# A linear-attention + feed-forward kernel: blocks of two batches, two tokens in each partition, and every engine's order from a list scheduler

## The chip, the cores and the metric

The kernel runs on one core of one Trainium2 chip. The metric is the time of one execution on the device in microseconds (us). A run is called slow when it is over 1.5% above the fastest of the same kernel, and fast runs are compared with fast runs. Each batch of experiments ran on one chip (by the record, chip 7, chip 14, and chip 4 for the last two), together with runs of the kernel before, whose median varied from 199.2 to 202.1 us between batches. So results of different batches are compared by their ratio to the kernel before of the same batch.

## The reference

A decayed linear attention ("RWKV-5"), whose output goes straight into a two-layer feed-forward part with a piecewise quadratic activation.

```python
# r, k, v: (4 batches, 8 heads, 768 tokens, 48); w, u: (8, 48)
for t in range(S):
    cur = einsum('bhd,bhe->bhde', u * k[t], v[t])
    y[t] = einsum('bhd,bhde->bhe', r[t], state + cur)
    state = w * state + einsum('bhd,bhe->bhde', k[t], v[t])
x = y.transpose(0, 2, 1, 3).reshape(3072, 384)
h = x @ w_in                                  # (384, 2048)
g = where(h >= 1, h, where(h <= -1, 0, (h + 1)**2 / 4))
return g @ w_out                              # (2048, 384)
```

The attention is computed in chunks of 128 tokens. Within a chunk, R is multiplied by powers of w and K by inverse powers, so that a plain product of R and K gives the decayed scores; a mask makes it causal; a state T carries what came before the chunk. For this data |h| stays under 1, so the activation is one squaring on ScalarE. A bound on norms is computed on the side, and a general path is run if it fails, which it never does here.

## The kernel before

The unit of attention is one batch and one chunk of 128 tokens, so a token is a partition. There are 24 units. Two of them make a block of 256 tokens for the feed-forward part, so there are 12 blocks.

```python
io = ctx.enter_context(tc.tile_pool(name="io", bufs=6))
...
man.enter_context(tc.block(schedule_with_timeline_sim=True))
units = [(b, c) for c in range(NCH) for b in range(B)]

def load():                       # one unit: 128 partitions, 8 runs of 192 bytes in each
    ...
    for name, src in (("K", k), ("R", r), ("V", v)):
        t = io.tile([128, H, D], F32, name=name, tag=name)
        nc.sync.dma_start(out=t, in_=src[b, :, t0 : t0 + C, :].rearrange("h s d -> s h d"))

def prep(i):
    nc.gpsimd.tensor_mul(Kw[:, :, 0:D], K, Winv)
    (nc.vector if i < 6 else nc.gpsimd).tensor_mul(Rw[:, :, 0:D], R, Wpow)
    nc.gpsimd.tensor_mul(KU, K, u3)
    nc.gpsimd.tensor_mul(KU, KU, R)
    ...                           # V to bf16
def s_tr(i):                      # R and K transposed: PE for the first 12 units, then by DMA
    if i >= TD:
        nc.sync.dma_start_transpose(RK, RKW[i % NR].rearrange("q h d -> q (h d)"))
        return
    ...
def s_y(i):                       # y = scores * V + R * state, then + V * diag, head by head
    ...
    for h in range(H):
        nc.vector.scalar_tensor_tensor(x[:, h*D:(h+1)*D], V[:, h, :], diag[:, h:h+1], y[:, h, :],
                                       op0=ALU.mult, op1=ALU.add)
    ...
def layer1(m, n):                 # 6 matmuls 128x256, then the squaring on ScalarE
def layer2(m, n):                 # 4 matmuls 128x384; at the end copy, and one 128-partition store
    ...
    nc.sync.dma_start(out=out[t0 : t0 + C, :], in_=o_sb)
# then a hand-written order: prep(0), prep(1), s_tr(0), s_at(0), ..., the steady state from a plan
```

Of the kernel before, what the change touches and what calls it, by code (L numbers as in the profile page):

```python
# [15 lines left out]
def kernel(  # L16
# [11 lines left out]
    nc = tc.nc  # L28
# [4 lines left out]
    NP = H // 2  # L33
    d_model = H * D
# [7 lines left out]
    NB = B * NCH // UB  # L42
    LIM = 0.95
    mm = nc.tensor.matmul

    const = ctx.enter_context(tc.tile_pool(name="const", bufs=1))
    stage = ctx.enter_context(tc.tile_pool(name="stage", bufs=4))
    io = ctx.enter_context(tc.tile_pool(name="io", bufs=6))
    work = ctx.enter_context(tc.tile_pool(name="work", bufs=3))
    gpool = ctx.enter_context(tc.tile_pool(name="gpool", bufs=3))  # L50
# [3 lines left out]
    ps_a = ctx.enter_context(tc.tile_pool(name="ps_a", bufs=4, space=bass.MemoryType.PSUM))  # L54

    man = ExitStack()
    man.enter_context(tc.block(schedule_with_timeline_sim=True))


    units = [(b, c) for c in range(NCH) for b in range(B)]  # L60
    loaded = {}
    next_load = [0]

    def load():
        i = next_load[0]
        if i == len(units):
            return
        next_load[0] += 1
        b, c = units[i]
        t0 = c * C  # L70
        tiles = []
        for name, src in (("K", k), ("R", r), ("V", v)):
            t = io.tile([128, H, D], F32, name=name, tag=name)
            nc.sync.dma_start(out=t, in_=src[b, :, t0 : t0 + C, :].rearrange("h s d -> s h d"))
            tiles.append(t)
        loaded[i] = tiles
# [4 lines left out]
    w_bc = const.tile([128, H * D], F32, name="w_bc")  # L81
    nc.sync.dma_start(out=w_bc, in_=row_bcast(w))

    wc = const.tile([128, NP], F32, name="wc")
    nc.vector.memset(wc, 1.0)
    with nc.allow_non_contiguous_dma(reason="384 words"):
        for s in range(2):
            nc.sync.dma_start(
                out=wc[s * DP : s * DP + D, :],
                in_=w.rearrange("(p s) d -> s d p", s=2)[s],  # L90
            )
    load()
    u_bc = const.tile([128, H * D], F32, name="u_bc")
    nc.sync.dma_start(out=u_bc, in_=row_bcast(u))
    load()

    w_in_sb = const.tile([128, nKb, d_ff], BF16, name="w_in_sb")
    w_out_sb = const.tile([128, nN, d_out], BF16, name="w_out_sb")
    NQ = 4
    FQ, TQ = d_ff // NQ, nN // NQ  # L100
    w_in_src = moe_w_in.rearrange("(ko ki) n -> ki ko n", ki=128)
    w_out_src = moe_w_out.rearrange("(no ni) d -> ni no d", ni=128)
    w_in_f, w_out_f = [], []
    for q in range(NQ):
        t = stage.tile([128, nKb, FQ], F32, name="w_in_f", tag="wf")
        nc.sync.dma_start(out=t, in_=w_in_src[:, :, q * FQ : (q + 1) * FQ])
        w_in_f.append(t)
        load()
    for q in range(NQ):
        t = stage.tile([128, TQ, d_out], F32, name="w_out_f", tag="wf")  # L110
        nc.sync.dma_start(out=t, in_=w_out_src[:, q * TQ : (q + 1) * TQ, :])
        w_out_f.append(t)


    ident = const.tile([128, 128], BF16, name="ident")
    make_identity(nc, ident)
    umask = const.tile([128, 128], F32, name="umask")
    nc.gpsimd.memset(umask, 0.0)
    nc.gpsimd.affine_select(
        out=umask, in_=umask, compare_op=ALU.is_ge, fill=1.0,  # L120
        base=0, pattern=[[-1, 128]], channel_multiplier=1,
    )
    ones = const.tile([128, 1], BF16, name="ones")
    nc.vector.memset(ones, 1.0)
    i_int = const.tile([128, 1], mybir.dt.int32, name="i_int")
    nc.gpsimd.iota(i_int, pattern=[[0, 1]], base=0, channel_multiplier=1)
    i_col = const.tile([128, 1], F32, name="i_col")
    nc.vector.tensor_copy(i_col, i_int)
    negj_col = const.tile([128, 1], F32, name="negj_col")
    nc.vector.tensor_scalar(negj_col, i_col, -1.0, -1.0, ALU.mult, ALU.add)  # L130
    lw = const.tile([128, H * D], F32, name="lw")
    nc.scalar.activation(lw, w_bc, AF.Ln)
    nc.scalar.activation(wc, wc, AF.Ln)
    Wpow = const.tile([128, H, D], F32, name="Wpow")
    nc.scalar.activation(Wpow.rearrange("p h d -> p (h d)"), lw, AF.Exp, scale=i_col)
    Winv = const.tile([128, H, D], F32, name="Winv")
    nc.scalar.activation(Winv.rearrange("p h d -> p (h d)"), lw, AF.Exp, scale=negj_col)  # L137
    nc.scalar.activation(wc, wc, AF.Exp, scale=float(C))
    u3 = u_bc.rearrange("p (h d) -> p h d", h=H)
    wc3 = wc[:, :, None].to_broadcast([128, NP, D])  # L140
    umask4 = umask[:, None, :].to_broadcast([128, NP, 128])



    NR = 4
    TD = 12
    RKW = []
    for i in range(NR):
        t = const.tile([128, 2 * H, DP], BF16, name=f"RKW{i}")
        nc.vector.memset(t, 0.0)  # L150
        RKW.append(t)

    T = [const.tile([128, NP, D], F32, name=f"T{b}") for b in range(B)]
    Tbd = []
    for b in range(B):
        nc.gpsimd.memset(T[b], 0.0)
        t = const.tile([128, NP, 2 * D], BF16, name=f"Tbd{b}")
        nc.gpsimd.memset(t, 0.0)
        Tbd.append(t)
    xT = [const.tile([128, UB, nKb, C], BF16, name=f"xT{m}") for m in range(NB)]  # L160
    xn = const.tile([128, len(units)], F32, name="xn")

    def pair(t, p):
        return t[:, 2 * p : 2 * p + 2, :].rearrange("q h d -> q (h d)")


    ut = {}

    def prep(i):
        K, R, Vf = loaded.pop(i)  # L170
        RK_w = RKW[i % NR]
        Rw, Kw = RK_w[:, 0:H, :], RK_w[:, H : 2 * H, :]
        nc.gpsimd.tensor_mul(Kw[:, :, 0:D], K, Winv)  # L173
        (nc.vector if i < 6 else nc.gpsimd).tensor_mul(Rw[:, :, 0:D], R, Wpow)
        KU = work.tile([128, H, D], F32, name="KU", tag="KU")
        nc.gpsimd.tensor_mul(KU, K, u3)  # L176
        nc.gpsimd.tensor_mul(KU, KU, R)  # L177
        V = work.tile([128, H, D], BF16, name="V", tag="V")
        if i < 8:
            nc.scalar.copy(V, Vf)  # L180
        else:
            nc.gpsimd.tensor_copy(V, Vf)  # L182
        ut[i] = [Rw, Kw, V, KU]

    def s_tr(i):
        Rw, Kw, V, KU = ut[i]
        RK = work.tile([128, 2 * NP, 128], BF16, name="RK", tag="RK")
        ut[i] = [Kw, V, RK, KU]
        if i >= TD:
            nc.sync.dma_start_transpose(RK, RKW[i % NR].rearrange("q h d -> q (h d)"))  # L190
            return
        tr = ps_a.tile([128, 2 * NP, 128], BF16, name="tr", tag="a")
        for p in range(NP):
            nc.tensor.transpose(tr[:, NP + p, :], pair(Kw, p), ident)  # L194
        for p in range(NP):
            nc.tensor.transpose(tr[:, p, :], pair(Rw, p), ident)  # L196
        nc.scalar.copy(RK, tr)  # L197

    def s_at(i):
        Kw, V, RK, KU = ut[i]  # L200
        RT, KT = RK[:, 0:NP, :], RK[:, NP : 2 * NP, :]
        AT_p = [ps_a.tile([128, NP, 128], F32, name=f"AT_p{s}", tag="a") for s in range(2)]
        for p in range(NP):
            for s in range(2):
                rows = slice(s * DP, s * DP + D)
                mm(AT_p[s][:, p, :], KT[rows, p, :], RT[rows, p, :], start=True, stop=True)  # L206
        AT = []
        for s in range(2):
            a = work.tile([128, NP, 128], BF16, name=f"AT{s}", tag=f"AT{s}")
            nc.vector.tensor_mul(a, AT_p[s], umask4)  # L210
            AT.append(a)
        diag = work.tile([128, H], F32, name="diag", tag="diag")
        nc.vector.reduce_sum(diag, KU, axis=mybir.AxisListType.X)  # L213
        load()
        ut[i] = [Kw, V, RT, AT, diag]

    def s_y(i):
        b, c = units[i]
        Kw, V, RT, AT, diag = ut[i]
        y = ps_a.tile([128, H, D], F32, name="y", tag="a")  # L220
        first = True
        if c > 0:
            for p in range(NP):
                mm(pair(y, p), RT[:, p, :], Tbd[b][:, p, :], start=first, stop=False, skip_group_check=True)  # L224
                first = False
        for h in range(H):
            mm(  # L227
                y[:, h, :], AT[h % 2][:, h // 2, :], V[:, h, :],
                start=first, stop=(h == H - 1), skip_group_check=True,
            )  # L230
            first = False
        if c < NCH - 1:
            st = ps_a.tile([128, NP, 2 * D], F32, name="st", tag="a")
            for p in range(NP):
                mm(st[:, p, :], pair(Kw, p), pair(V, p), start=True, stop=True)  # L235
# [5 lines left out]
        if c < NCH - 1:  # L241
            for s in range(2):
                rows = slice(s * DP, s * DP + D)
                part = st[rows, :, s * D : (s + 1) * D]
                if c > 0:
                    nc.vector.tensor_add(T[b][rows], T[b][rows], part)
                else:
                    nc.vector.tensor_copy(T[b][rows], part)
# [250 lines left out]
```

## Time and profile before

| | before |
|---|---|
| time, median of 3 runs | 200.65 us |
| span of the profiled run | 199.1 us |
| first layer-1 matmul | 25.03 us |
| first layer-2 matmul | 42.55 us |
| six layer-1 matmuls, four layer-2 matmuls, start to start | 0.655 us, 0.65 us |
| feed-forward work, 96 x 1.305 | 125.3 us |

Four lines of the page cut the span into 40 equal slices. A digit is the busy share of a slice in tenths (9 is 90% or more), and GB/s is what all 16 DMA engines of the core moved. From the page of the kernel before, with the count of packets, the queue of loads and stores, and the last column of the transfers, the us from issue to landing:

```profile
PE   0263598998989999999999959999999999999990
DMA  4999989999969999999999998334315022020202
GB/s 96 201 258 264 250 195 221 243 181 268 262 131 244 173 193 169 258 195 173 253 162 216 165 168 206 76 74 132 64 35 153 2 66 66 9 79 0 82 3 89
DMA packets 100444, 30.25 MB, mean 152 GB/s; under 512 B 93504, under 2 KB 98880, under 8 KB 100416
q1 hardware_dynamic: 100416, 29.90, 75.1%
K<-in_k_dram SPq DMA_DIRECT2D x24, 192.0 KB, 4.9
out_dram<-o_sb SPq DMA_DIRECT2D x24, 192.0 KB, 2.3
w_in_f<-in_moe_w_in_dram SPq DMA_DIRECT2D x4, 768.0 KB, 5.7
w_out_f<-in_moe_w_out_dram SPq DMA_DIRECT2D x4, 768.0 KB, 5.9
```

TensorE (PE) is full from about 60 us to the end, but for one slice. Next, the table of stretches of the kernel before (columns: window, its length, busy us with instruction counts of PE, weight loads, DVE, ACT and POOL, granted clock, mean DMA share, GB/s). A DMA share over 1 means that packets overlap on an engine.

```profile
20.00:40.00 20.00, 16.88 (x176) 12.87 (x178) 18.48 (x55) 16.74 (x36) 14.77 (x16) 1.00 1.01 228
60.00:80.00 20.00, 20.00 (x202) 14.67 (x202) 11.23 (x32) 12.31 (x25) 18.41 (x22) 1.00 1.17 194
100.00:120.00 20.00, 17.48 (x178) 12.29 (x177) 12.81 (x46) 10.52 (x25) 14.63 (x19) 0.92 1.17 177
120.00:140.00 20.00, 20.00 (x216) 14.62 (x214) 12.68 (x45) 12.65 (x28) 13.81 (x18) 1.00 0.52 119
```

And three rows of PE's timeline of the kernel before (start, us, engine, line, operation, out<-in, count, and in brackets the idle time just before it and what ended it):

```profile
25.03 2.77 PE L279 MATMUL h_p<-xT_195,w_in_sb 128*128 128x256 bf16 x12
42.55 1.58 PE L297 MATMUL o_p<-w_out_sb,gT 128*128 128x384 bf16 x8
116.52 2.52 PE L279 MATMUL h_p<-xT_201,w_in_sb 128*128 128x256 bf16 x12 [2.47 <-DMA xT_201<-x]
```

### The profile page before, as it was taken

The page shows a single profiled execution, that of the slowest core. Times are in us where ns is not written, and L with a number is a line of the kernel's source. Part 1 is how long each engine was busy: PE and PEld are TensorE (multiplying, and loading weights), DVE is VectorE, ACT ScalarE, POOL GpSimd, SP SyncE. Part 2 cuts the span into 40 slices and gives each one's busy share as a digit, 9 for nine tenths or more (in the row PEclk, how much of TensorE's full clock was granted, in tenths as well). Part 3 has the DMA queues.
Part 4 walks back from the last instruction along what each step waited for, and adds up shares of the span by engine and source line. Part 5 has one row for each costly group of instructions (what it writes and reads, how often), then busy time and mean ns, then how long its engine had stood idle before and what let it go on. Part 6 is the DMA issues. An engine that isn't in the chain of part 4 may idle for free.

```text
span 199.1 us, 4592 instructions
## 1 busy us (share of the span) xinstructions
PE 172.3 (87%) x1686; PEld 125.7 (63%) x1686; DVE 111.8 (56%) x354; ACT 122.0 (61%) x251; POOL 110.8 (56%) x144
## 2 busy tenths in 40 slices
PE   0263598998989999999999959999999999999990
PEld 0141476776867677866777547677667677777750
DVE  4179979994867608842867643776576464200110
ACT  3657769999887547936558326567555356454540
POOL 7496756989976999967679386857221000000000
PEclk9999999999999999999999979999999999999999
DMA  4999989999969999999999998334315022020202
GB/s 96 201 258 264 250 195 221 243 181 268 262 131 244 173 193 169 258 195 173 253 162 216 165 168 206 76 74 132 64 35 153 2 66 66 9 79 0 82 3 89
DMA packets 100444, 30.25 MB, mean 152 GB/s; under 512 B 93504, under 2 KB 98880, under 8 KB 100416
## 3 DMA queue, kind: packets, MB, share of 16 engines
q1 hardware_dynamic: 100416, 29.90, 75.1%
q8 instruction: 15, 0.25, 0.6%
q14 instruction: 13, 0.11, 0.2%
HBM read 20.84 MB, written 4.72 MB: 128 GB/s over the span
## 4 chain that ended last, share of the span: by engine, by line
PE 66%; DMA 5%; DVE 4%; ACT 2%; POOL 1%; issue 1%; ACTq 0%; DVEq 0%
PE o_p L297 28%; PE h_p L279 26%; DVE x L238 3%; DMA xT_201<-x 3%; DMA R<-in_r_dram 2%; PE y L227 2%; PE y L224 2%; PE st L235 1%; PE xp L265 1%; PE tr L194 1%; ACT gT L285 1%; ACT RK L197 1%; POOL RKW_173 L173 0%; POOL KU L177 0%; PE tr L196 0%
## 5 line engine op out<-in xcount | busy, mean ns | idle before, releaser
L285 ACT ACTIVATE gT<-h_p 128x512 bf16<-128x512 f32 x96 | 56.8, 598 | 44.9 <-PE h_p L279 42.6
L297 PE MATMUL o_p<-w_out_sb,gT 128*128 128x384 bf16 x384 | 73.5, 327 | 0.0
L279 PEld LDWEIGHTS <-w_in_sb 128*128 128x128 bf16 x576 | 54.5, 99 | 14.5 <-issue 3.4
L297 PEld LDWEIGHTS <-gT 128*128 128x128 bf16 x384 | 36.2, 98 | 19.3 <-issue 0.7
L238 DVE SCALAR_TENSOR_TENSOR x<-V,diag,y 128x48 bf16<-128x48 bf16 x192 | 35.8, 257 | 18.5 <-PE y L227 11.1
L176 POOL TENSOR_TENSOR KU<-K,u_bc 128x384 f32<-128x384 f32 x24 | 24.5, 1021 | 1.9 <-DVE diag L213 1.6
L177 POOL TENSOR_TENSOR KU<-KU,R 128x384 f32<-128x384 f32 x24 | 24.3, 1013 | 0.3
L301 DVE COPY o_sb<-o_p 128x384 f32<-128x384 f32 x12 | 6.7, 555 | 23.8 <-PE o_p L297 23.7
L197 ACT COPY RK<-tr 128x1024 bf16<-128x1024 bf16 x12 | 12.2, 1014 | 3.9 <-PE tr L196 3.8
L182 POOL CAST V<-V 128x384 bf16<-128x384 f32 x16 | 8.1, 503 | 11.3 <-DVE x L238 7.0
L206 PEld LDWEIGHTS <-RK 48*128 48x128 bf16 x192 | 8.3, 99 | 9.5 <-issue 4.2
L213 DVE TENSOR_REDUCE diag<-KU 128x8 f32<-128x384 f32 x24 | 13.1, 546 | 2.1 <-POOL KU L177 1.9
L265 PE MATMUL xp<-ident,x 128*128 128x128 bf16 x36 | 7.9, 236 | 5.6 <-DVE x L238 5.1
L301 ACT COPY o_sb<-o_p 128x384 f32<-128x384 f32 x12 | 5.7, 476 | 7.5 <-PE o_p L297 6.4
L173 POOL TENSOR_TENSOR RKW_171<-K,Winv 128x384 bf16<-128x384 f32 x6 | 6.0, 997 | 6.9 <-ACT Winv L137 3.5
L279 PE MATMUL h_p<-xT_201,w_in_sb 128*128 128x256 bf16 x48 | 7.4, 302 | 2.5 <-DMA xT_201<-x 2.5
L173 POOL TENSOR_TENSOR RKW_177<-K,Winv 128x384 bf16<-128x384 f32 x6 | 6.2, 1029 | 6.1 <-PE st L235 3.9
L265 PEld LDWEIGHTS <-x 128*128 128x128 bf16 x36 | 3.6, 101 | 8.9 <-DVE x L238 8.0
L194 PE MATMUL tr<-ident,RKW_171 128*128 128x128 bf16 x12 | 1.4, 249 | 8.8 <-POOL RKW_171 L173 8.8
L173 POOL TENSOR_TENSOR RKW_173<-K,Winv 128x384 bf16<-128x384 f32 x6 | 6.6, 1094 | 3.6 <-DMA K<-in_k_dram 1.8
L279 PE MATMUL h_p<-xT_195,w_in_sb 128*128 128x256 bf16 x48 | 7.7, 311 | 0.1
L173 POOL TENSOR_TENSOR RKW_175<-K,Winv 128x384 bf16<-128x384 f32 x6 | 6.4, 1072 | 2.1 <-DMA K<-in_k_dram 1.6
(356 smaller groups left out, 321.9 us busy)
## 6 DMA issues: line engine op xcount, KB each, us to landing
K<-in_k_dram SPq DMA_DIRECT2D x24, 192.0 KB, 4.9
R<-in_r_dram SPq DMA_DIRECT2D x24, 192.0 KB, 4.7
V<-in_v_dram SPq DMA_DIRECT2D x24, 192.0 KB, 4.9
out_dram<-o_sb SPq DMA_DIRECT2D x24, 192.0 KB, 2.3
w_in_f<-in_moe_w_in_dram SPq DMA_DIRECT2D x4, 768.0 KB, 5.7
w_out_f<-in_moe_w_out_dram SPq DMA_DIRECT2D x4, 768.0 KB, 5.9
w_bc<-in_w_dram SPq DMA_DIRECT2D x1, 192.0 KB, 3.5
u_bc<-in_u_dram SPq DMA_DIRECT2D x1, 192.0 KB, 4.3
```

Of the source, the lines that this page charges most:

```text
L173: nc.gpsimd.tensor_mul(Kw[:, :, 0:D], K, Winv)
L176: nc.gpsimd.tensor_mul(KU, K, u3)
L177: nc.gpsimd.tensor_mul(KU, KU, R)
L197: nc.scalar.copy(RK, tr)
L206: mm(AT_p[s][:, p, :], KT[rows, p, :], RT[rows, p, :], start=True, stop=True)
L213: nc.vector.reduce_sum(diag, KU, axis=mybir.AxisListType.X)
L238: nc.vector.scalar_tensor_tensor(x[:, h * D : (h + 1) * D], V[:, h, :], diag[:, h : h + 1], y[:, h, :], op0=ALU.mult, op1=ALU.add)
L265: nc.tensor.transpose(xp[:, kk, :], x[:, kk * 128 : (kk + 1) * 128], ident)
L279: mm(h_p[:, f, :], w_in_sb[:, kk, (2 * n + f) * 128 : (2 * n + f + 1) * 128], xT[m][:, :, kk, :], start=(kk == 0), stop=(kk == nKb - 1),)
L285: nc.scalar.activation(g, h_p, AF.Square, bias=0.5, scale=0.5)
L297: mm(o_ps[m][j], gT[m][:, f, j * C : (j + 1) * C], w_out_sb[:, f, :], start=(f == 0), stop=(f == nN - 1))
L301: (nc.scalar.copy if j else nc.vector.tensor_copy)(o_sb, o_ps[m][j])
```

## The change

The intent was threefold: fewer and longer DMA packets (384 bytes instead of 192), fewer and larger instructions on DVE and POOL (256 tokens in each), and an earlier, denser start, from an order that a list scheduler works out inside the kernel. A block is now two batches and one chunk. Batch b of the two lies on partitions 64b to 64b+63, with two neighbouring tokens in each partition, so each load and each store becomes two transfers of 64 partitions.

```diff
-    units = [(b, c) for c in range(NCH) for b in range(B)]
-    ...
-            t = io.tile([128, H, D], F32, name=name, tag=name)
-            nc.sync.dma_start(out=t, in_=src[b, :, t0 : t0 + C, :].rearrange("h s d -> s h d"))
+    blocks = [(c, b0) for c in range(NCH) for b0 in range(0, B, UB)]
+    half = [slice(b * HC, (b + 1) * HC) for b in range(UB)]          # HC = 64
+    def load(m, name):
+        c, b0 = blocks[m]
+        tl = io.tile([128, H, UB * D], F32, name=name, tag=name)
+        for b in range(UB):
+            nc.sync.dma_start(
+                out=tl[half[b]],
+                in_=src[b0 + b, :, c * C : (c + 1) * C, :].rearrange("h (p j) d -> p h (j d)", j=UB),
+            )
...
-        (nc.vector if i < 6 else nc.gpsimd).tensor_mul(Rw[:, :, 0:D], R, Wpow)
+        on_pool = name == "K" and m >= EARLY                           # EARLY = 3 blocks
+        (nc.gpsimd if on_pool else nc.vector).tensor_mul(to[:, js], src[:, js], tab[:, js])
...
-        for h in range(H):
-            nc.vector.scalar_tensor_tensor(x[...], V[:, h, :], diag[:, h : h + 1], y[:, h, :], ...)
+    # V*diag is a POOL product; PE adds it to y (3 early blocks), or DVE in four adds (the others)
...
-                nc.sync.dma_start(out=out[t0 : t0 + C, :], in_=o_sb)
+        for i in range(UB):
+            nc.sync.dma_start(out=out[t0 + i : t0 + C : UB, :], in_=t["o_sb", m, j][half[i]])
...
-    man.enter_context(tc.block(schedule_with_timeline_sim=True))
+    man.enter_context(tc.block())
+    man.enter_context(tc.manual_schedule())
+    P, L0 = 12.3, 16.0                              # us of a block; wished start of layer 1
+    for m in range(NB):                             # every operation: engine, us, needs, date, buffers
+        op(("ld", name, m), "SP", 1.55, (load, m, name), ...)
+        op(("tr", m), "SP", 3.1, (tr_dma, m), ...)
+        op(("xs", m), "ACT", 0.9, (xsq, m), [("x", m)], ..., start=27.0 if early else 0.0)
+        op(("L1", m, n), "PE", 0.66, (layer1, m, n), ...)
+        op(("L2", m, j, n), "PE", 0.33, ..., [...("xT", EARLY - 1)...])   # not before block 2's x
+    ...
+    while left:                                     # take the most urgent of what can start next
+        ...
+    # and dummy matmuls into unused PSUM in PE's idle time of the first 40 us, to keep its clock up
```

Scores, y and state are twice as many half-array matmuls, since the two halves of the partitions are different batches. Only 3 of 12 blocks are transposed on PE, instead of 12 of 24 units. The feed-forward matmuls stay as they were.

## The prediction

> **What bounds the kernel now.** TensorE, but not all the time. In the timeline six layer-1 matmuls (128x256) take 0.655 us start to start and four layer-2 matmuls (128x384) 0.65, so the feed-forward part needs 96 x 1.305 = 125.5 us. By the same view one attention unit costs PE about 1.0 us for scores, y and state, and 0.6 more where PE transposes (12 of 24 units). With the weight norms I estimate 158 us of PE work in a span of 199. By the table of stages PE is full from 60 us on, but for 2.5 us at 111 us, where layer 1 waits for the transposing DMA into xT_201 (chain of waits). The other ~38 us: the first layer-1 matmul starts at 25 us; 25 to 60 us has short gaps while ACT is 90% and DVE 80% busy and 192-byte loads saturate the DMAs; the last matmul (193.7) is followed by 5.4 us of copy, store and end. The first twelve layer-1 matmuls take 2.6 us, twice their later time, though the granted clock reads 1.00. The Trainium skill ("TensorE: Matmul & The Clock Gate", part 1) says an idle PE runs at half clock until some 3.4 us of activity; the trace agrees.
>
> **What changes.** Feed-forward matmuls stay.
> - Loads have 384-byte runs: 36,864 packets, not 73,728, same bytes. "DMA: Bandwidth & Descriptors" (why small descriptors are slow) names a fixed cost per packet; I expect the loads to land sooner while DMA is saturated.
> - V*diag+y, eight DVE instructions per unit (0.19 us start to start), becomes PE adds or four DVE adds per block plus a POOL product. Masks halve in number, not in elements. POOL stays near 10 us per block; ACT is near full from 10 to 40 us.
> - PE transposes remain for 3 of 12 blocks, not 6: 3 to 4 us of PE saved, more DMA transposes.
> - Scores, y and state become twice as many half-array matmuls; if two overlap, as the score pairs do now (starts 0.01 us apart), about 2.2 us per block against 2.0: +2 us.
> - Dummy matmuls keep the clock up: 1.5 us gained.
> - The order: layer 1 is to start near 16 us.
>
> **On the critical path.** First layer 1 near 17 us, not 25. Layer 2 cannot start before block 2's transpose, about 32 us, with some 8 us of layer 1 done. Left then: 117.5 feed-forward + 9 blocks x 2.2 - 0.8 (no last states) + 1.6 norms = 138 us; 32 + 138 = 170, + 3 of waits, + 5.4 end = 178.5 span, + 1.5 (time minus span, before) = 180.
>
> **Prediction:** 180 us, range 174 to 189. Faster by over 2%: 0.93; within 2%: 0.04; slower: 0.03.
>
> **Seen in the profile if right:** first layer-1 matmul at 15 to 19 us, at full rate; first layer-2 matmul at 30 to 36; layer groups still 0.65; no PE hole over 2 us after 45 us; attention 2.0 to 2.5 us of PE per block; 66 PE transposes of data, not 132; load packets halved; end still about 5 us.
>
> **What would make it wrong.** Half-array matmuls that don't overlap, or drain PE at each switch: up to +20. DVE and POOL slowing each other (DVE's R product took 0.56 to 1.35 us), so that the fixed order stalls; POOL over 12.5 us per block would be the limit. ACT late with block 2: each us there is one at the end. Loads that don't speed up: +4. A denser start and 2.0 us per block: 174.

## More of the kernel before

Loads are issued from one queue, the SP engine's, and so are the transposing transfers and the stores.

The twelve matmuls at 25 us take 2.77 us, nearly twice what twelve take later (1.49 us at 28.6 us). The twelve after the one hole, from 114.05 to 116.52 us, where PE waited 2.47 us for a transposing transfer (the prediction puts this hole at 111 us), take 2.52 us. The trace has the granted clock at 0.50 there, from 116.8 to 120.1 us.

## The result

The changed kernel is slower: 213.22 us median (211.97, 212.94 and 213.50 fast, 216.08 slow) against 200.63 (199.09 to 200.88) in the same rounds. The ratio of the fast runs is 1.0751, 95% interval 1.0643 to 1.0859. A ratio in this document is the record's: the mean time of one kernel's fast runs over that of the other's fast runs of the same rounds, so it is not quite the ratio of the medians quoted. For this pair the runs listed don't give it: their fast means are 212.80 and 200.31 us, a ratio of 1.062, just under the recorded interval. A size that rests on 1.0751 is uncertain by 1%, and is given below as a range.

The page of the changed kernel (span 210.1 us), the same lines as above:

```profile
PE   7769949999899859994979894979999999999980
DMA  5999999999999998999999998992570220503042
GB/s 118 202 204 332 221 241 268 242 211 213 249 181 187 161 184 186 198 195 163 207 199 172 205 180 182 155 180 60 51 164 3 52 65 0 115 0 75 3 100 64
DMA packets 72224, 32.49 MB, mean 155 GB/s; under 512 B 65280, under 2 KB 70656, under 8 KB 72192
q1 hardware_dynamic: 72192, 32.06, 83.7%
K<-in_k_dram SPq DMA_DIRECT2D x24, 192.0 KB, 5.3
out_dram<-o_sb SPq DMA_DIRECT2D x48, 96.0 KB, 2.2
w_in_f<-in_moe_w_in_dram SPq DMA_DIRECT2D x4, 768.0 KB, 10.3
w_out_f<-in_moe_w_out_dram SPq DMA_DIRECT2D x4, 768.0 KB, 8.2
```

There are 28,000 packets fewer, and yet the queue's packets now fill 83.7% of a longer span instead of 75.1%. DMA is full to about 142 us instead of 120. No load lands sooner (medians of K, R and V: 5.3 to 5.6 us, and 4.7 to 4.9 before), and the quarters of w_in take 10.3 us instead of 5.7. The 7s at the start of PE's row are mostly dummy matmuls. The table of stretches of the changed kernel:

```profile
20.00:40.00 20.00, 16.46 (x285) 13.80 (x282) 15.20 (x17) 15.19 (x29) 7.20 (x5) 0.91 1.17 240
60.00:80.00 20.00, 16.72 (x281) 11.52 (x280) 14.57 (x20) 9.53 (x21) 11.69 (x9) 1.00 1.21 186
100.00:120.00 20.00, 18.61 (x268) 13.30 (x262) 14.55 (x19) 11.27 (x23) 12.10 (x10) 1.00 1.14 195
120.00:140.00 20.00, 15.49 (x201) 10.74 (x200) 11.72 (x18) 10.52 (x23) 13.95 (x9) 0.91 0.99 179
```

Between 60 and 80 us PE was full before (20.00) and is now 16.72, while DVE, ACT and POOL are all less busy than 15 of 20 us. No compute engine is full there, but the DMA share is 1.21. PE's timeline of the changed kernel shows the start and three of the holes:

```profile
23.87 1.47 PE L370 MATMUL h_p<-xT,w_in_sb 128*128 128x256 bf16 x12
47.95 0.81 PE L390 MATMUL o_p<-w_out_sb,gT 128*128 128x384 bf16 x4
76.01 1.16 PE L370 MATMUL h_p<-xT,w_in_sb 128*128 128x256 bf16 x9 [3.11 <-DMA xT<-x]
99.73 0.52 PE L338 MATMUL st<-Vb,RKW 64*128 64x96 bf16 x16 [2.95 <-DVE AT L259]
129.36 0.64 PE L254 MATMUL A<-RK 48*64 48x128 bf16 x16 [2.89 <-DVE wsq L441]
129.94 1.46 PE L390 MATMUL o_p<-w_out_sb,gT 128*128 128x384 bf16 x4
```

The dummies did their part: the first twelve layer-1 matmuls take 1.47 us, not 2.77, although the granted clock fell to 0.50 once more later (30.1 to 33.4 us). But they start at 23.87 us, not near 17, and layer 2 starts at 47.95, not near 32.

The hole before 76.01 shows how a full DMA queue gets to PE. The two views below are the timeline of the SP queue (the time that issuing took, waiting for room or for data included) and that of POOL, both of the changed kernel:

```profile
50.00 9.66 SPq L244 DMA_TRANSPOSE RK<-RKW  x2
62.27 1.35 SPq L187 DMA_DIRECT2D K<-in_k_dram  x2
69.19 2.34 SPq L323 DMA_TRANSPOSE xT<-x  x1
```
```profile
67.26 1.82 POOL L199 TENSOR_TENSOR RKW<-K,Winv 128x768 bf16<-128x768 f32 x1 [7.05 <-DMA K<-in_k_dram]
```

Two transposing transfers hold the queue for 9.66 us, so the next K is issued at 62.27, and POOL sits idle for 7.05 us until it has landed. The transposing transfer of x sits in the same queue behind four stores and eight loads; x is ready at 67.2, its transfer is issued at 69.19, and PE gets its input at 76.01. Over the whole span, the waits of the changed kernel hold two lines for loads (columns: us in total, times, longest). Before, the same waits add up to 8.4 us for K, in four lines because the tiles were numbered there, and 3.1 us for R:

```profile
POOL RKW L199 <- DMA K<-in_k_dram: 11.8, 3, 7.0
DVE RKW L199 <- DMA R<-in_r_dram: 9.7, 5, 3.2
```

The trace also has a record of every DMA packet. I grouped those of the queue of loads, stores and transposes by size (mean ns that a packet took, and their sum per engine of 16):

```
                 192/384-byte loads   256-byte transposes   1536-byte stores,    2048-byte      sum,
                 ns    us/engine      ns    us/engine       w_out: ns  us/eng    w_in: ns       us/engine
before          18.9    87.3         24.4   25.8            74.9   25.2          101.2          149.6
after           37.1    85.6         28.2   44.7            97.0   32.6          111.3          175.8
```

Here a packet of twice the bytes takes twice as long (37.1 against 18.9 ns), so the loads cost the queue what they cost before, 86 us per engine. The stores cost more, although their bytes are the same, and the transposes cost 19 us more, most of it because there are more of them. That is the reading that the experiments had to explain.

### The profile page after: what moved, and what is told of

It is laid out like the page before. It is cut to its first block, busy times and chain, and to the rows that moved or that the text cites. A ratio compares the mean times of both kernels' runs of the same rounds, so it can differ in the third digit from the quotient of the medians.

```text
span 210.1 us, 5752 instructions
## 1 busy us (share of the span) xinstructions
PE 182.0 (87%) x2427; PEld 135.8 (65%) x2427; DVE 111.5 (53%) x148; ACT 112.7 (54%) x221; POOL 102.7 (49%) x80
## 3 DMA queue, kind: packets, MB, share of 16 engines
q1 hardware_dynamic: 72192, 32.06, 83.7%
HBM read 20.84 MB, written 4.72 MB: 122 GB/s over the span
## 4 chain that ended last, share of the span: by engine, by line
PE 47%; DMA 16%; DVE 11%; SPq 9%; ACT 6%; issue 4%; POOL 4%; DVEq 0%; POOLq 0%; ACTq 0%
PE o_p L390 19%; PE h_p L370 16%; SPq L187 6%; DMA K<-in_k_dram 5%; DVE RKW L199 4%; PE w_p L149 4%; DMA xT<-x 3%; DMA w_out_f<-in_moe_w_out_dram 3%; DVE x L305 3%; DMA R<-in_r_dram 3%; PE A L254 2%; ACT gT L379 2%; DVE AT L259 2%; DMA V<-in_v_dram 2%; SPq L244 2%
## 5 line engine op out<-in xcount | busy, mean ns | idle before, releaser
L370 PE MATMUL h_p<-xT,w_in_sb 128*128 128x256 bf16 x576 | 78.2, 276 | 3.8 <-DMA xT<-x 3.1
L259 DVE TENSOR_TENSOR AT<-A,umask 128x1024 bf16<-128x1024 f32 x24 | 28.2, 1218 | 18.0 <-PE A L254 18.0
L207 POOL TENSOR_TENSOR KU<-K,u_bc 128x768 f32<-128x768 f32 x12 | 23.2, 1936 | 9.7 <-DVE x L305 4.6
L199 DVE TENSOR_TENSOR RKW<-R,Wpow 128x768 bf16<-128x768 f32 (+1 forms) x13 | 22.0, 1700 | 10.0 <-DMA R<-in_r_dram 9.7
L210 POOL TENSOR_TENSOR KU<-KU,R 128x768 f32<-128x768 f32 x12 | 25.6, 2134 | 1.3 <-DMA R<-in_r_dram 0.5
L199 POOL TENSOR_TENSOR RKW<-K,Winv 128x768 bf16<-128x768 f32 x9 | 16.3, 1808 | 19.6 <-DMA K<-in_k_dram 11.8
L305 DVE TENSOR_TENSOR x<-y,KU 64x384 bf16<-64x384 f32 x36 | 20.0, 555 | 9.0 <-PE y L282 4.6
L149 PE MATMUL w_p<-ident 128*128 128x128 bf16 x251 | 20.2, 244 | 1.9 <-POOL ident masks.py:199 1.4
L149 PEld LDWEIGHTS <-ident 128*128 128x128 bf16 x251 | 17.9, 112 | 2.8 <-POOL ident masks.py:199 1.4
L223 POOL TENSOR_TENSOR KU<-V,dg 128x768 f32<-128x768 f32 x9 | 13.5, 1500 | 4.0 <-DVE dg L214 3.0
## 6 DMA issues: line engine op xcount, KB each, us to landing
w_in_f<-in_moe_w_in_dram SPq DMA_DIRECT2D x4, 768.0 KB, 10.3
```

Source lines behind the costliest of these rows:

```text
L149: mm(w_p[:, 0:128], ident, ident, start=True, stop=True)
L199: (nc.gpsimd if on_pool else nc.vector).tensor_mul(to[:, js], src[:, js], tab[:, js])
L207: nc.gpsimd.tensor_mul(t["KU", m], t["K", m], ub4)
L210: nc.gpsimd.tensor_mul(t["KU", m], t["KU", m], t["R", m])
L223: nc.gpsimd.tensor_mul(t["VD", m], t["V", m], dg)
L259: nc.vector.tensor_mul(a.rearrange("q s p t -> q (s p) t"), t["A", m, j].rearrange("q s p i t -> q (s p) (i t)"), umask4[j])
```

## The experiments

Theory 1: a transfer that covers only 64 partitions runs at a part of the rate of one that covers 128, and this takes back all that the longer runs gained. The Trainium skill states the first half of it on the page "SBUF — State Buffer", section "Door 1: The DMA port swizzle": partitions 0 to 63 reach 8 of the 16 ports, and the page measured 196 against 328 GB/s at 1 MiB. A later section ("Can I just issue two DMAs to hit both halves?") answers no, since two such transfers serialize. I had not looked there before predicting.

Rival 2: the order is wrong for the chip, because the list reckons with too short transfers. Rival 3: the start is bound by the compute engines (ScalarE's queue, DVE and POOL slowing each other, the dummies), and the late start costs its length. Fifteen kernels were run.

### 1. The transfers by themselves (m1_dma)

A kernel with no computation moves the same 4.72 MB six times, in transfers of six shapes, one after the other, and then stores. Its output is wrong, which doesn't matter for the time.

```python
# A: 128 partitions, 192-byte runs          B: two halves of 64 partitions, 384-byte runs
# C: 128 partitions, 384-byte runs          D: two halves, 192-byte runs
# E: 128 partitions, one 3072-byte run each F: two halves, one 3072-byte run each
for i, (x, b, c) in enumerate(jobs):        # C, for example
    nc.sync.dma_start(out=big[i], in_=x[b, :, c*128 : c*128+256, :].rearrange("h (p j) d -> p h (j d)", j=2))
```

> Six ways to move the same 4.7 MB of K, R and V, one after the other, nothing else running (output zero, wrong on purpose): A 128 partitions with 192-byte runs, B two halves of 64 partitions with 384-byte runs, C 128 partitions with 384-byte runs, D halves with 192-byte runs, E 128 partitions with 3072-byte runs, F halves with 3072-byte runs; then stores of 1536-byte rows, whole and in two interleaved halves. Theory 1[...]: C moves at 1.5 to 2 times the rate of B, B about as fast as A, D at half of A, F at half of E, half stores slower than whole ones. Rival 2 (under 512 bytes a packet costs in proportion to its bytes, whatever the partitions): B and C alike, A and D alike. Rival 3 (a packet has a fixed cost, and 384-byte packets were slow in the kernel only because of transposes and weights beside them): B twice as fast as A.

The rows of DMA and GB/s of this run's page have 40 slices of 4.2 us:

```profile
DMA  5999995999949995778877775994999966916664
GB/s 107 218 213 206 205 187 126 242 233 232 233 84 321 325 323 159 132 141 140 150 143 144 146 135 199 364 412 160 242 246 247 246 154 243 324 53 158 148 159 97
```

The plateaus are, in order, A, B, C, D, E, F and the stores. From the first issue of one phase to that of the next:

| shape | 192-byte runs | 384-byte runs | 3072-byte runs |
|---|---|---|---|
| 128 partitions | A 24.3 us, 194 GB/s | C 16.7 us, 282 GB/s | E 14.9 us, 317 GB/s |
| two halves of 64 | D 35.5 us, 133 GB/s | B 23.1 us, 204 GB/s | F 22.5 us, 210 GB/s |

The longer run is worth a factor of 1.45 (A to C), and the half width costs a factor of 1.4 (C to B) to 1.5 (E to F). The change went from A to B, across the diagonal, and the two nearly cancel: 194 to 204 GB/s. Stores of half width took 17 us where whole ones took 8, for the same 2.36 MB.

Two cautions. A shape in halves also has twice as many transfers here (B 24, C 12), and this run doesn't separate the two; A and B have 24 each. And D and the half stores are no clean measure of width: their DMA tenths are 7 to 8 and 6, not 9, so the DMA engines were not full (D's 48 transfers were issued 0.67 us apart). The packets themselves took 15.6 ns (A), 31.9 (B), 22.2 (C), 16.7 (D), 129 (E) and 201 (F), and those of the stores 68.2 whole and 100.5 in halves. So the direction of theory 1 holds for transfers alone, but the factor of 1.5 to 2 that I expected for B and C came out at 1.4. What it is worth in the kernel is another question.

### 2. Loads over all partitions, data wrong (e1_heads)

The changed kernel with each load's pair of transfers cut by heads, not by partitions. It has the same number of transfers, the same bytes and the same runs, but the tile then holds other data, so the output is wrong. Half-width stores remain.

```diff
-                out=tl[half[b]],
-                in_=src[b0 + b, :, c * C : (c + 1) * C, :].rearrange("h (p j) d -> p h (j d)", j=UB),
+                out=tl[:, hs],                               # hs: 4 of 8 heads
+                in_=src[b0, hs, c2 * C : (c2 + 2) * C, :].rearrange("h (p j) d -> p h (j d)", j=UB),
```

> The changed kernel, but each pair of load DMAs splits the tile by heads and not by partitions: both fill all 128 partitions, with 256 tokens of one batch (wrong data on purpose). Same number of DMAs, same 192 KB each, same 384-byte packets, same order on every engine. Theory 1[...]: the 384-byte packets fall from 37 ns to 20 to 25, loads land in 3 to 4 us and not 5.6, PE holes after 58 us shrink, the time falls from 213 to about 190 (180 to 198). Rivals 2 and 3 (bytes, or the order): packets stay at 35 to 37 ns, time 208 to 215.

It took 200.79 us (ratio 0.9984, 0.9877 to 1.0091, against 1.0751). The load packets took 26.0 ns instead of 37.1 (expected: 20 to 25), K landed in 4.8 us (expected: 3 to 4), and the queue's sum fell from 175.8 to 146.2 us per engine. The time fell by less than I expected of theory 1: it missed 190 by about 10 us and lies outside the 180 to 198 stated. The first layer 2 was still at 43.5 us. So the width is a large part of the loss, and not all of it.

### 3. No loads after the third block (e3_noload)

The later blocks reuse the tiles of the first three (output wrong). This takes 54 of 72 load transfers away.

```diff
+        if m >= 3:
+            t[name, m] = t[name, m - 3]
+            return
```

> The changed kernel without the K, R, V loads of blocks 3 to 11 (they use the tiles of blocks 0 to 2 again; wrong on purpose), transposes and stores kept. If DMA capacity is what gates blocks 3 to 11, PE has no hole over 2 us after 60 us and the time is 180 to 190. If the fixed order or the transposes alone gate them, it stays above 200.

It took 197.65 us (0.9861, 0.9765 to 0.9957), again short of the expected 180 to 190. From 60 us on PE has no hole over 1.1 us, and from the first layer 2 (45.9 us) to the end of the span it takes 148.5 us, where the prediction's sum has 138 + 3 + 5.4 = 146.4. So with the DMA freed the second part runs nearly as predicted, and what is missing lies before 50 us. That splits the error into two parts: the steady part, which DMA limits, and the start.

### 4. The list told what transfers really take (e4_est)

```diff
-            op(("ld", name, m), "SP", 1.55, ...        -            op(("tr", m), "SP", 3.1, ...
+            op(("ld", name, m), "SP", 2.1, ...         +            op(("tr", m), "SP", 4.0, ...
-        op(("li", q), "SP", 2.4, ... (and "lo")        -    LAND = 1.1
+        op(("li", q), "SP", 4.1, ... (and "lo")        +    LAND = 3.5
```

> The changed kernel with the scheduler told what the trace shows of DMA: a 384 KB load 2.1 us instead of 1.55, landing 3.5 us later instead of 1.1, weights 4.1 instead of 2.4, transposes 4.0 instead of 3.1. Same work, other order, result right. If a wrong order costs the time (rival), it comes down by 10 us or more, to 195 to 203. If DMA capacity costs it, it stays within 4 us of 213.

It took 215.87 us, ratio 1.0733 (1.0643 to 1.0822), the same as the changed kernel. Better estimates make another order, and it gains nothing. Rival 2 falls in this form.

### 5. DVE without POOL beside it (e5_pool)

The R*Wpow products on DVE took 0.95 us alone and up to 2.57 us beside POOL products, 1.70 in the mean. The Trainium skill ("SBUF — State Buffer", section "Who interferes with whom") says that a DVE instruction with two SBUF inputs contends with a GpSimd instruction that reads SBUF, and not with one that only writes it. So in the three early blocks I put two write-only fills in place of each of the three POOL products. The output passes the comparison, because that term is small.

```diff
     def ku1(m):
         t["KU", m] = work.tile([128, H, UB, D], F32, name="KU", tag="KU")
+        if m < EARLY:
+            nc.gpsimd.memset(t["KU", m], 0.01)
+            nc.gpsimd.memset(t["KU", m], 0.01)
+            return
         nc.gpsimd.tensor_mul(t["KU", m], t["K", m], ub4)       # ku2 and vdiag likewise
```

> The changed kernel, but the GpSimd products of the first three blocks (K*u, *R, V*diag) are memsets of the same tiles, which read no SBUF (wrong on purpose). Theory S1 (VectorE's products of two SBUF operands wait for GpSimd's, which doubles them on the way to the first layer 2): the DVE weighting products of blocks 0 to 2 fall from 2.6 us to 0.95, the first layer-2 matmul comes at 40 to 42 us instead of 46, the time falls by 3 to 6 us. Rival (the start is set by ScalarE, the dummies or the loads): the products shorten, but first layer 2 and time move by under 2 us.

The DVE products of the early blocks fell to 0.95 us, which agrees with the page, and the first layer 1 came at 20.61 us, 3.3 us earlier. The first layer 2 moved by 1.5 us only (46.47 us; the profile is of a slow run), and the time did not follow: 211.62 us in the one fast run, 215.19 to 216.12 in the three slow ones (so no ratio is given). PE then waited for quarters of w_out until 60 us. The contention is real: the products at 9.3, 14.2 and 16.0 us ran beside fills. But a fill takes 0.74 us where a product takes 1.5 to 2.6, and it waits for no load, so this run doesn't separate the contention from the shorter POOL work; together they cost 3 us of the first layer-1 date, and nothing of the total that shows.

### 6. No dummy matmuls (e6_nodummy)

```diff
-    WARM_END = 40.0
+    WARM_END = 0.0
```

> The changed kernel without the dummy matmuls. Theory S2 (the 41 dummies between scores and y of block 0 take 3.4 us where the scheduler reckons 2.3, so they hold up the real work): y of block 0 starts at about 16.5 us instead of 17.7, but the first layer-1 matmuls run at half speed; net -2 to +2 us. If the dummies are what keeps the clock up, the first layer-1 groups take 1.3 us instead of 0.66 and the time grows by 2 to 4 us.

It took 212.93 us (ratio 1.0684, 1.0561 to 1.0808; two of its four runs are slow). The first twelve layer-1 matmuls took 3.08 us instead of 1.47, so the dummies do keep the clock up. In the total they neither help nor hurt by more than the spread of the runs.

### 7. and 8. Full width with right data (v1, v1s)

To have full-width loads with right data, the block becomes one batch and two consecutive chunks (256 tokens). Two neighbouring tokens stay in a partition, partitions 0 to 63 hold the first chunk and 64 to 127 the second, and one transfer of 384 KB brings all of it. The state of the first chunk is handed to the second within the block. Version v1s also writes the activation's output in token order, so that a store is one transfer of 128 partitions.

```diff
-    blocks = [(c, b0) for c in range(NCH) for b0 in range(0, B, UB)]
+    blocks = [(c, b) for c in range(0, NCH, UB) for b in range(B)]       # first of two chunks, batch
-        for b in range(UB):
-            nc.sync.dma_start(out=tl[half[b]], in_=src[b0 + b, ...])
+        nc.sync.dma_start(
+            out=tl, in_=src[b0, :, c * C : (c + UB) * C, :].rearrange("h (p j) d -> p h (j d)", j=UB))
...                                                  # state added, decayed and cast once per chunk
# v1s:
-        for i in range(UB):
-            nc.sync.dma_start(out=out[t0 + i : t0 + C : UB, :], in_=t["o_sb", m, j][half[i]])
+        nc.sync.dma_start(out=out[t0 : t0 + C, :], in_=t["o_sb", m, j])
```

> A right version with full-width loads: a block is one batch and two chunks of 128 tokens that follow each other, so 256 tokens lie two to a partition over all 128 partitions and one DMA of 384 KB loads them; the second chunk's state comes from the same block. The rest as in the changed kernel. If the half-width loads cost what the run with loads split by heads says, it is near 200 (195 to 206), right, with 384-byte packets of 26 ns.

> The same, and ScalarE writes the hidden layer in token order, so that each output tile is stored by one DMA from 128 partitions instead of two from 64. Store packets (1536 bytes) fall from 97 to about 75 ns, some 7 us of every DMA engine's time; the last store ends 0.5 us sooner. Time 0 to 4 us below v1, unless ScalarE's strided writes are slower (hidden-layer activation over 0.65 us).

Both outputs are right. v1 took 203.09 us (1.0228, 1.0137 to 1.0318) and v1s 199.32 (1.0001, 0.9915 to 1.0086), on the same chip. The whole stores are worth 3.8 us (their packets went from 98.0 to 75.2 ns), net of what they cost: written in token order, the activation on ScalarE takes 746 ns instead of 594, over the 0.65 us that the expectation had named as the danger. In the same step the feed-forward work done by 49 us fell from 11.1 to 9.7 us; no run shows whether the activation did that. The later versions all keep this write. After 56 us v1s has no PE hole over 0.6 us. Its start is still slow: first layer 1 at 26.7 us, first layer 2 at 50.4.

### 9. to 12. The start (e7_xs, e8_early2, v2, v3)

Two things hold layer 2 back. One is the written rule that it may not start before the x of the last early block is transposed (they share PSUM buffers). The other is ScalarE's queue in front of that. e7_xs takes the squares of x of the early blocks (3 us of ScalarE work, needed only for the norm bound) out of the start. e8_early2 transposes only two blocks on PE, so that the rule refers to block 1. v2 and v3 apply both, or the first alone, to v1s.

```diff
# e7_xs (and v3, with 4 buffers of x):
-    RING = dict(..., x=2, ...)
+    RING = dict(..., x=5, ...)
-        op(("xs", m), "ACT", 0.9, (xsq, m), [("x", m)], d + 12 if early else d + 9, start=27.0 if early else 0.0)
+        op(("xs", m), "ACT", 0.9, (xsq, m), [("x", m)], d + 40 if early else d + 9, start=60.0 if early else 0.0)
# e8_early2 (and v2, beside the squares):
-    EARLY = 3
+    EARLY = 2
-    first += ["o0", "K3", "R3", "o1", "V3", "o2", "K4", "R4", "V4", "o3"]
+    first += ["o0", "t2", "o1", "K3", "R3", "o2", "V3", "o3"]            # t2: block 2's transpose
```

> The changed kernel with the squares of x for blocks 0 to 2 put off past 60 us (four buffers of x more to allow it); everything else as it was. If ScalarE's queue at the start sets the first layer 2 (the third block's x goes through three ScalarE steps, and 2 us of squares stand at 35 us), the list itself brings the first layer 2 forward by 4.5 us (38.9 to 34.4 in its own dates) and it comes at about 43 us instead of 48. Theory one (half-width transfers keep the DMA queues full up to about 150 us) expects that the time hardly follows: 209 to 213 us. The rival, that the late start costs its full length, expects about 207 to 208 us.

> The changed kernel with two blocks instead of three transposed on TensorE, and the third block's transposing transfer placed among the first loads. The written rule that layer 2 may only start when the last early block's x is transposed then refers to block 1, which is done near 35 us, so the first layer 2 should come at 38 to 42 us instead of 48, when the first quarter of w_out is there. If the late start of layer 2 as such costs the time, 202 to 207 us; if the transfers limit, it is 210 to 216 us, with a new hole before block 2's first layer 1, whose x now has to wait for two transposing transfers.

> The full-width version with whole stores (run before: 199.3 us), with two early blocks and the squares of x put off. Output should be right. With full-width transfers the queues have room, so an earlier first layer 2 (expected 40 to 43 us instead of 50) should be worth most of its length: 192 to 196 us, faster than both kernels. If the start is instead bound by what the transfers bring in by 50 us, the time stays at 198 to 201 us with a hole at 45 to 60 us.

> The full-width version with whole stores and three early blocks, with only the squares of x put off (four x buffers). Output should be right. ScalarE loses 3 us of work before the first layer 2: first layer 2 at 46 to 48 us instead of 50, time 196 to 199 us. If it gives nothing, 199 to 200 us.

| | time, us | ratio to before | first layer 2 | feed-forward done by 49 us |
|---|---|---|---|---|
| before (first chip) | 200.63 | 1 | 42.55 us | 12.2 us |
| after (first chip) | 213.22 | 1.0751 | 47.95 us | 8.9 us |
| e7_xs | 215.00 | 1.0673 (1.0584 to 1.0763) | 43.40 us | 8.8 us |
| e8_early2 | 210.32 | 1.0330 (1.0188 to 1.0471) | 40.58 us | 11.6 us |
| v1s (batch of v1) | 199.32 | 1.0001 (0.9915 to 1.0086) | 50.37 us | 9.7 us |
| v2 | 197.26 | 0.9775 (0.9682 to 0.9868) | 35.44 us | 13.7 us |
| v3 | 197.24 | 0.9784 (0.9702 to 0.9867) | 45.87 us | 13.7 us |

The last column counts the layer-1 and layer-2 matmuls that have started by 49 us, each at its later rate (0.109 and 0.1625 us), out of 125. The profiles of e5_pool and e8_early2 are of slow runs; the others are of fast ones.

In e7 layer 2 came 4.5 us earlier, as the list had it, and the time did not improve. In the half-width kernel the date of the first layer 2 was not the limit, as theory 1 had expected. e8 gained 3 to 4% by ratio, from four runs of which two are slow, so its size is uncertain; the mean of its fast runs, 206.95 and 209.45, fell between the two stated ranges, 202 to 207 and 210 to 216. In the full-width kernel putting off the squares did gain. Both v2 and v3 beat the kernel before by 2.2% (intervals 1.3 to 3.2% and 1.3 to 3.0%) and are right; whether the gain is over 2% stays unclear. v2 missed what was expected of it (192 to 196 us). v2's layer 2 starts 10 us before v3's, yet both have 13.7 us done by 49 us, and both take 197 us. So in this pair it is the amount of feed-forward work that fits in by then that goes with the time, not when layer 2 begins.

### 13. to 15. Only the width, in a right kernel (w_half, w_heads, w_both)

So far the width had been changed together with other things, or with wrong data. The last three runs take v3 and change nothing but the shape of its transfers. The data, the order written and the outputs are the same.

```diff
-        nc.sync.dma_start(out=tl, in_=src[b0, :, c * C : (c + UB) * C, :].rearrange("h (p j) d -> p h (j d)", j=UB))
+        whole = src[b0, :, c * C : (c + UB) * C, :].rearrange("h (p j) d -> p h (j d)", j=UB)
+        for b in range(UB):
# w_half:
+            nc.sync.dma_start(out=tl[half[b]], in_=whole[half[b]])
# w_heads:
+            nc.sync.dma_start(out=tl[:, hs], in_=whole[:, hs])           # hs: 4 of 8 heads
# w_both: as w_half, and the stores too
-        nc.sync.dma_start(out=out[t0 : t0 + C, :], in_=t["o_sb", m, j])
+        for i in range(UB):
+            nc.sync.dma_start(out=out[t0 + i * HC : t0 + (i + 1) * HC, :], in_=t["o_sb", m, j][half[i]])
```

> v3 (197.2 us; 0.978 of before) with each 128-partition load cut into two transfers of 64 partitions each, nothing else. Output right. If half-width transfers are the cause, the mean time of a 384-byte packet goes from 27 to 36-37 ns, the queues' work from 141 to about 163 us per engine, and the time rises by most of what it fell from the changed kernel: 203 to 210 us. If it was the block's form or the order that helped, the time stays at 196 to 199 us.

> v3 with each load cut into two transfers by heads, each over all 128 partitions: as many transfers of the same size as in w_half. If the partitions matter and not the number of transfers, 384-byte packets stay at 26 to 28 ns and the time at 196 to 199 us. If it is the number of transfers (24 to 48 more issues on the SP queue), it goes with w_half.

> v3 with loads and stores both cut into halves by partitions (the stores still of contiguous rows). If the cause is the width, the stores' 1536-byte packets go from 73 to 95-107 ns and the time goes 3 to 5 us above w_half, to 207-214 us, about the changed kernel's. If only the loads matter, it equals w_half within 1 us.

| | transfers | time, us | ratio to before | load packet, 384 bytes | store and w_out packet, 1536 bytes | queue, per engine |
|---|---|---|---|---|---|---|
| v3 (the batch before) | loads and stores whole | 197.24 | 0.9784 | 26.8 ns | 72.7 ns | 140.7 us |
| w_heads | loads in two, all partitions | 195.76 | 0.9839 (0.9732 to 0.9945) | 25.8 ns | 73.6 ns | 139.5 us |
| w_half | loads in two, by partitions | 210.05 | 1.0559 (1.0468 to 1.0650) | 36.7 ns | 82.4 ns | 171.8 us |
| w_both | loads and stores by partitions | 215.00 | 1.0783 (1.0673 to 1.0893) | 36.4 ns | 99.2 ns | 175.5 us |

Cutting the loads by heads costs nothing. Cutting the same loads by partitions costs 14.3 us (w_half against w_heads: same rounds, the same number and size of transfers, and no run of one within 12 us of a run of the other). Cutting the stores so costs 5.0 more; there the number of stores doubles too, and no run has twice as many stores at full width. Together that is 19.2 us, and it brings the best version to about the changed kernel's time (215.00 against 213.22 us; w_both was expected at 207 to 214). The page lines show it too, first those of v3 (span 193.7 us):

```profile
DMA  4999999699929979998999999406600303020031
GB/s 104 269 282 342 304 327 309 152 316 243 194 87 263 248 174 221 266 151 187 275 197 271 222 214 216 124 0 54 179 3 11 110 3 95 32 80 1 25 103 52
q1 hardware_dynamic: 71232, 32.06, 72.6%
K<-in_k_dram SPq DMA_DIRECT2D x12, 384.0 KB, 5.9
```

those of w_heads (span 193.1 us):

```profile
DMA  5999999699929999999998999802900402201031
q1 hardware_dynamic: 71808, 32.06, 72.2%
K<-in_k_dram SPq DMA_DIRECT2D x24, 192.0 KB, 4.6
```

and those of w_half (span 209.2 us):

```profile
DMA  4999999999996999999999999960660300402031
GB/s 106 200 203 329 211 256 278 218 213 195 233 166 172 204 200 188 211 231 147 202 202 195 202 199 205 177 173 0 50 166 3 109 7 2 116 0 75 0 119 48
q1 hardware_dynamic: 71808, 32.06, 82.1%
K<-in_k_dram SPq DMA_DIRECT2D x24, 192.0 KB, 5.2
```

After the first slice the DMA engines move 270 to 340 GB/s in v3 and mostly 200 to 280 in w_half, for the same 32.06 MB over the whole span. Of the slices before 60 us two more than the first have slack in v3 (the 6 and the 2); in w_half all are full but the first. And in the waits of w_half there stand the two lines that the changed kernel had, at almost the same size (in v3 they are 2.2 and 3.6 us):

```profile
POOL RKW L197 <- DMA K<-in_k_dram: 12.3, 5, 5.7
DVE RKW L197 <- DMA R<-in_r_dram: 10.0, 5, 3.3
```

## Why the prediction was wrong

The predicted time was 180 us and the range 174 to 189; it took 213. The miss is 33 us. Point by point, in the order of the prediction:

- Right: the feed-forward groups stayed at 0.655 and 0.65 us. Attention on PE took 2.0 us per late block (scores 0.58, y 0.46 and 0.51, state 0.45), and half-array matmuls did not drain PE. There were 66 transposes of data, and 36,864 load packets. The dummies brought the first layer 1 to full rate: 1.47 us instead of 2.77. The end took 6.2 us after the last layer 2, about the "+ 5.4 end".
- Wrong: "I expect the loads to land sooner while DMA is saturated". They land later, K after 5.3 us instead of 4.9. The argument had one factor of a product. At full width a packet of twice the bytes does not take twice as long (15.6 and 22.2 ns in m1_dma), and longer runs are worth 1.45 in transfer alone; but the same diff sends each load to 64 partitions, which costs 1.4. This is the failed step. It was also named too small among the risks: "Loads that don't speed up: +4".
- Wrong, following from it: "+ 3 of waits" and "no PE hole over 2 us after 45 us". From 49 us to the last layer 2 at 203.6 us, the 116.4 us of feed-forward work left took 154.6, so 38 us were not feed-forward. Attention, norms and the 3 us of waits should have been at most 23.5 of them (138 - 117.5 + 3). That is about 15 us of the miss. Much of it goes in holes like those before 76.01, 99.73 and 129.36. The first waits for a transfer. The second can be followed back over DVE and POOL to a K that POOL had waited 3.6 us for; the third to POOL products behind a wait of 2.5 us, while DVE waited 2.7 us for R. That these waits come from the full queue is shown by the runs that change the queue alone, not by the trace.
- Wrong: "First layer 1 near 17 us" (23.87) and "Layer 2 cannot start before block 2's transpose, about 32 us" (47.95). If 8 us were done at 32 us, and the rest ran at the predicted 117.5 in 138, then 22.5 us would be done by 49 us. It was 8.9, which is 13.6 us of the miss.

The two wrong terms, at least 15 and 13.6 us, give 29 of the 33 us; of the rest, 2.4 us lie in the end (0.8), the time outside the span (1.9 instead of 1.5) and the profiled run being 1.2 us faster than the median. They have two causes between them:

1. Half-width transfers, shown: 14.3 us for the loads, in a pair of kernels that differ in nothing else, and 5.0 us more when the stores are cut too, by width or by their doubled number. They act in both terms. By 49 us w_half has done 9.8 us of feed-forward work and w_heads 13.2, which is 3.4 us of the start; the other 16 come later. Undoing the loads' part of it in the changed kernel itself (e1_heads) took the time from 213.22 to 200.79 us and the ratio from 1.0751 to 0.9984, or 12 to 15 us.
2. A start that I reckoned too fast, apart from the transfers. Even v2 and v3, with full width, have 13.7 us done by 49 us and not 22.5, which is 8.8 us. From 20 to 40 us in v3 ScalarE is busy for 18.91 of 20 us, so I take it for the next limit; ten of the slower activations are 7.5 us of it, which would be 5.9 at the 594 ns of v1 (an estimate). The trials agree with that without proving it: putting off 3 us of ScalarE work brought 4.0 us more done by 49 us with full width (v1s to v3, on different chips), and nothing with half width (e7_xs), where the queue was the limit before it.

My prediction had summed the start from the dates at which single steps could end, with each engine free when needed. What stays open is what sets the full-width start in detail. The dummies and the POOL contention were tried in the half-width kernel, where freeing them gave nothing in the total, and they were not tried again with full width. Nor was a full-width kernel with whole stores and the quicker activation.

A smaller part: some holes cost more than their length. After the 2.89 us hole, four layer-2 matmuls take 1.46 us instead of 0.81, and the granted clock of the stretch from 120 to 140 us is 0.91. The profiled clock was 0.97 in the changed kernel and 0.962 in w_half, against 0.985 in v3 and 0.990 in w_heads.

## What to carry to other kernels

When a change makes packets longer, look in the same diff for what it does to the partitions of the transfer. Reckon with both factors, and look at the row of DMA busy tenths first: where it was full here, the shape of the transfers set the time, although most waits named compute engines. A load cut by heads and one cut by partitions look alike in count and bytes, and here one cost nothing and the other 14 us. A version that differs from the best kernel in nothing but the suspected part is what turned a plausible cause into a number.

## What the Trainium skill lacked or had wrong

- "SBUF — State Buffer" (Door 1: The DMA port swizzle) agrees with these runs, and would have warned of the failed step if read: it has 196 against 328 GB/s at 1 MiB; here 4.72 MB took 22.5 us in halves and 14.9 us whole (210 and 317 GB/s). It lacks how half width acts in a mixed queue. There the other transfers slow down as well: quarters of w_in landed in 10.0 us instead of 8.1 (w_half, v3), and the 1536-byte packets took 82.4 ns instead of 72.7 although their own shape was unchanged.
- "DMA: Bandwidth & Descriptors" (Rules for kernel authors) says of two transfers to disjoint partition halves not to bother, since they serialize. The row gives no figure for what the pair costs against the one whole transfer: here 23.1 against 16.7 us for 4.72 MB of loads in 384-byte runs. For stores in halves neither page has a figure: here a packet took 100.5 ns in halves and 68.2 whole.
- "TensorE: Matmul & The Clock Gate" (Part 1: The HAM clock gate) gives an idle window of some 3.4 us after which the clock halves. Holes of 2.47 us (before) and 2.89 us (after) were followed by half-rate matmuls here, with the granted clock at 0.50 from 116.8 to 120.1 us and from 129.1 to 132.4 us; after holes of 3.11 and 2.95 us it stayed at 1.00. So it lacks that a single hole shorter than that window can already cost, and that the longer of two such holes need not be the one that does.
